# Strips of 64 bytes between the eight w_in slots of an attention and two-MLP kernel

## The chip, the cores and the metric

The kernel runs on one core of one Trainium2 chip. Its time is device microseconds of one execution, as the median of several runs. The engines go by their names in the profile: PE (TensorE matmuls), PEld (its weight loads), DVE (VectorE), ACT (ScalarE), POOL (GpSimd), SP (the queue that issues the DMAs).

## The reference

```python
proj = einsum('bhsd,df->bhsf', x, w_phi); proj -= max(abs(proj), axis=-1)
phi  = concat([exp(proj), exp(-proj)])                  # for q and for k
out  = (phi(q) @ (phi(k).T @ v)) / (phi(q) @ sum(phi(k)) + 1e-6)
x    = out as 2304 tokens x 512
x    = elu(x @ w1_in) @ w1_out                          # 512 -> 2048 -> 512
x    = (h * clip(h + 3, 0, 6) / 6) @ w2_out,  h = x @ w2_in
```

The batch is 4, with 8 heads, 576 positions and a head of 64. The weights of the MLPs arrive as 64-bit floats and are turned into 32-bit ones on the chip.

## The kernel before

The first 160 us or so are the attention, in eight units of two heads by two batches. Then come the two MLPs. Each MLP runs in eight rounds over its 2,048 hidden features, 256 features per round; the rounds are called 0 to 7 (first MLP, m = 0) and 8 to 15 (second, m = 1), and `g` is the round in the code. The 2,304 tokens are four blocks of 512 and one of 256.

A round computes the hidden layer of the four large blocks, two at a time, with Strassen's scheme in Winograd-like form: seven products P1 to P7 per pair of blocks instead of eight (`hid`, line 711). Each has an operand of the tokens (`X`, tiles x_A.. and x_S..) and one of the weights, a *part* of w_in: B11, B21, B12 and B22 are its quarters, T1 to T4 are sums and differences of these. The small block goes without the scheme and reads the four quarters (`hid4`, line 725). To keep precision, each operand is split into a high and a low half in the format fp32r, and a product is three matmuls (high by high, high by low, low by high); with two halves of the contraction that is a group of six matmuls of 128 x 128 weights against 512 columns. The second layer is `outp`, line 776, with w_out and the gated hidden tiles ga and gb.

A w_in part is one tile of 128 partitions by 2,048 bytes, high half first. ACT casts the high half (`part_hi`, line 665), POOL subtracts it from the 32-bit weights for the low half (`part_lo`, line 669). Before that the quarters come by DMA and go through a chain of ACT (627, 631), DVE (642, 648) and POOL (636, 652); the T parts are differences made by POOL in the place of the quarters' 32-bit copies (`diff`, line 658). The parts of a round are made during the round before it, always in the order B11, B21, B12, B22, T2, T3, T1, T4.

Behind a product on PE, ACT copies or activates it (733, 745, 746, 748), DVE adds and gates it (738, 752), ACT casts the gated tile's high half (`gate_hi`, 756), and DVE makes its low half (`gate_lo`, 759), which also frees the PSUM bank. `sums` (786, 788) adds the second layer's results into x.

The order of all work on all engines is written out by the kernel itself: it makes a list of steps with expected durations, and `in_order` simulates them with a plan of `rings` (how many buffers each ring has and which steps must be over before one is taken again) and emits the instructions in that order. Each engine executes its own list in that order. The tile framework gives the tiles their addresses and puts in the semaphore waits, according to which tile had the memory before. Within a round of the middle, PE's order is written out in the list `order`: the small block's groups and the rest of the round before, P1 and P2, P6, P5, P7 and so on of the first pair of blocks, mixed with second-layer groups, then those of the second pair, with P3 and P4 of the second pair last. These are the last readers of B22 and of T4 in a round.

The w_in parts live in the pool `wp`, as eight buffers of one tag, `wi`. Above it lie `stg` (the staging of the weights), `early` and the attention's `att_b`, whose memory the second pair's operands take later.

Of the kernel before, what the change touches and what calls it, by code (L numbers as in the profile page):

```python
# [8 lines left out]
F32 = mybir.dt.float32  # L9
I64 = mybir.dt.int64  # L10
F32R = mybir.dt.float32r
# [137 lines left out]
def attention_then_two_mlps(  # L149
# [44 lines left out]
    def step(engine, us, fn, **kw):  # L194
        s = Step(engine, us, fn, **kw)
        steps.append(s)
        return s
# [5 lines left out]
    rings = dict(BANKS)  # L203
# [17 lines left out]
    ctx.enter_context(tc.tile_pool(name="gap", bufs=1, side="right")).tile([128, 120], F32, name="gap_r")  # L221

    wp = ctx.enter_context(tc.tile_pool(name="wp", bufs=1))
    stg = ctx.enter_context(tc.tile_pool(name="stg", bufs=1))
    early = ctx.enter_context(tc.tile_pool(name="early", bufs=1))

# [16 lines left out]
    for i in range(2):  # L243
        t = apool.tile([128, R, 2, D + 1], F32, name=f"vb{i}")
# [312 lines left out]
    PARTS = ("B11", "B21", "B12", "B22", "T2", "T3", "T1", "T4")  # L557
# [31 lines left out]
    def y_open():  # L589
# [6 lines left out]
        "y": step("NONE", 0.0, y_open, after=y_users, rank=BEGIN),  # L596
        "n": step("NONE", 0.0, y_open, after=n_users, rank=BEGIN),
    }
    HB, YB = ["p0", "p1", "p2", "p3", "t1"], ["a0", "a1", "t0"]
    rings.update({"s": 2, "ca": 2, "bi": 4, "bo": 2, "wi": 8, "wo": 3, "h": len(HB), "y": len(YB),  # L600
                  "ma": 2, "mb": 2, "ga": 2, "gb": 2})
    nxt = {}

# [5 lines left out]
    F, WI, WO = {}, {}, {}  # L609
# [51 lines left out]
        nc.gpsimd.tensor_scalar(out=out_, in0=in_, scalar1=1.0, scalar2=0.0, op0=ALU.mult, op1=ALU.add)  # L661

    def part_hi(g, name, key):
        t = WI[g, name] = wp.tile([128, 2, 2, 128], F32R, tag="wi", name="w_in", bufs=8)
        nc.scalar.copy(out=t[:, 0].rearrange("p k f -> p (k f)"), in_=F[key])  # L665

    def part_lo(g, name, key):
# [110 lines left out]
    def sums(m, first_, b, d):  # L778
        t0, n = BLOCKS[b]
        ps = Y[b, d]  # L780
        part, ps = (xv[:, d, t0:t0 + n], ps[:, :n]) if m == 0 else (ov[:, t0 // 128 + d], ps)
        if first_:
            if b == 4:
                V.tensor_copy(out=part, in_=ps)
            else:
                nc.scalar.copy(out=part, in_=ps)  # L786
        else:
            V.tensor_tensor(out=part, in0=ps, in1=part, op=ALU.add)  # L788
# [72 lines left out]
    for g in range(2 * NP):  # L861
# [3 lines left out]
        h = [[("H", g, fi)] for fi in range(2)]  # L865
# [44 lines left out]
    PART, OUT, wi_tok, wo_tok = {}, {}, {}, {}  # L910
    chain = [None, None]

    def convert(key, lead):
        m, w, i, c = key
        ts_, ta, tb = Token("s"), Token("ca"), Token(("bi", "bo")[i])
        x = step("SP", 1.4, bind_(fetch, *key), takes=[ts_], rank=lead - 5, behind=[chain[0]] if chain[0] else [])
        chain[0] = x
        low, size, sign, up, end = to_f32(key)
        x = step("ACT", 0.95, low, after=[x], rank=lead, takes=[ta, tb], uses=[ts_])
        z = step("DVE", 0.45, sign, after=[x], rank=lead, port=True, uses=[ts_])  # L920
        x = step("POOL", 0.45, size, after=[x], rank=lead)
        x = step("DVE", 0.3, up, after=[x], rank=lead, port=True)
        return step("POOL", 0.75, end, after=[x, z], rank=lead, uses=[ta, tb]), tb

    for g in range(2 * NP):
        m, w = g // NP, 2 * (g % NP)
        lead = first[g] - W_IN_LEAD
        keys = {"B11": (m, w, 0, 0), "B21": (m, w, 0, 1), "B12": (m, w + 1, 0, 0), "B22": (m, w + 1, 0, 1)}
        done, tok, raw_ = {}, {}, {}

        def part(name, key, after, users):
            t = wi_tok[g, name] = Token("wi")
            hi = step("ACT", 0.40, bind_(part_hi, g, name, key), after=after, rank=lead, takes=[t], uses=users,
                      behind=[chain[1]] if chain[1] else [])
            chain[1] = hi
            lo = step("POOL", 0.75, bind_(part_lo, g, name, key), after=[hi], rank=lead, uses=users + [t])
            PART[g, name] = lo
            return lo

        for name, key in keys.items():  # L940
            raw_[name], tok[name] = convert(key, lead)
            done[name] = part(name, key, [raw_[name]], [tok[name]])

        def differ(out_, one, two, after):
            return step("POOL", 0.75, bind_(diff, keys[out_], keys[one], keys[two]), after=after, rank=lead,
                        uses=[tok[out_], tok[one], tok[two]])

        t1 = differ("B11", "B12", "B11", [done["B11"], raw_["B12"]])
        t3 = differ("B12", "B22", "B12", [done["B12"], raw_["B22"], t1])
        t2 = differ("B22", "B22", "B11", [done["B22"], t1, t3])  # L950
        t4 = differ("B21", "B21", "B22", [done["B21"], t2])
        part("T2", keys["B22"], [t2], [tok["B22"]])
        part("T3", keys["B12"], [t3], [tok["B12"]])
        part("T1", keys["B11"], [t1], [tok["B11"]])
        part("T4", keys["B21"], [t4], [tok["B21"]])
        lead = first_o[g] - W_OUT_LEAD
        for fi in range(2):
            t = wo_tok[g, fi] = Token("wo")
            for c in range(2):
                x, tb = convert((m, w + fi, 1, c), lead)  # L960
                hi = step("ACT", 0.40, bind_(out_hi, m, w + fi, c), after=[x] + ([OUT[g, fi]] if c else []),
                          rank=lead, takes=[] if c else [t], uses=[tb])
                OUT[g, fi] = step("POOL", 0.75, bind_(out_lo, m, w + fi, c), after=[hi], rank=lead, uses=[tb, t])
# [22 lines left out]
    def joined(g, pr, bank_, to, key, after, when):  # L986
        pt = ptok[g, pr, bank_]
        if to != bank_:
            ptok[g, pr, to] = Token("h")
        return step("DVE", 0.70, bind_(join, (g, pr, bank_), key, (g, pr, to)), after=after, rank=when,  # L990
                    takes=[ptok[g, pr, to]] if to != bank_ else [], uses=[pt, ptok[g, pr, to], mtok[key]])
# [9 lines left out]
    for x in order:  # L1001
        kind, g = x[:2]
# [3 lines left out]
        if kind == "P":  # L1006
# [11 lines left out]
            if term in ("P6", "P5", "P3"):  # L1018
                after.append(at[g, pr, {"P6": "s1", "P5": "s2", "P3": "s4"}[term]])
            s = step("PE", us, bind_(hid, ps, g, pr, term, term in OPENS), after=after, rank=clock, takes=takes,  # L1020
                     behind=behind, uses=[ptok[ps], wi_tok[g, part_]])
# [12 lines left out]
            if term in ("P1", "P2") and {"P1", "P2"} <= set(seen):  # L1034
                y = joined(g, pr, "Y", "Y", (g, b0, 0), [at[g, pr, "P2"], at[g, pr, "s1"]], when)
                finish(m, g, b0, 0, [y], (g, pr, "Y"), None, when)
            if term in ("P5", "P7") and {"P5", "P7"} <= set(seen):
                y = at[g, pr, "C22"] = joined(g, pr, "Z", "W", (g, b1, 1), [at[g, pr, "P7"], at[g, pr, "s4"]], when)
                finish(m, g, b1, 1, [y], (g, pr, "W"), None, when)
            if term == "P4":  # L1040
                y = joined(g, pr, "Z", "Z", (g, b1, 0), [s, at[g, pr, "s2"]], when)
                finish(m, g, b1, 0, [y], (g, pr, "Z"), None, when)
        elif kind == "H":
            fi = x[2]
            ps = (g, 4)
            if fi == 0:
                ptok[ps] = Token("h")
            names = ("B11", "B21", "B12", "B22")[2 * fi:2 * fi + 2]
            s = step("PE", us, bind_(hid4, ps, g, fi), after=[PART[g, n_] for n_ in names] + ready[m, 4, None] + [OPEN["n"]],
                     rank=clock, takes=[] if fi else [ptok[ps]], behind=behind,  # L1050
                     uses=[ptok[ps]] + [wi_tok[g, n_] for n_ in names])
# [3 lines left out]
        else:  # L1055
# [3 lines left out]
            s = step("PE", us, bind_(outp, m, g, b, d), rank=clock, behind=behind, takes=[ty],  # L1059
                     after=[tiles[g, b, fi] for fi in fis] + [OUT[g, 0], OUT[g, 1], OPEN["y"], OPEN["n"]],  # L1060
                     uses=[ty, wo_tok[g, 0], wo_tok[g, 1]] + [gtok[g, b, fi] for fi in fis])
            when = clock + us
            w = g % NP
            if w == 0:
# [9 lines left out]
                y = step("ACT" if b < 4 else "DVE", 0.57 if m or b < 4 else 0.35, bind_(sums, m, True, b, d), after=after, rank=when, uses=[ty])  # L1074
            else:
                y = step("DVE", 0.66 if m or b < 4 else 0.41, bind_(sums, m, False, b, d), after=[s, adds[m, b, d]], rank=when, uses=[ty])
# [24 lines left out]
def bind_(fn, *a):  # L1101
    return lambda: fn(*a)
# [50 lines left out]
```

## Time and profile before

| | |
|---|---|
| median of 3 runs | 938.45 us (938.14 to 939.03) |
| the profiled execution | 938.99 us, of which the span of the instructions is 937.2 us |
| PE busy | 903.2 us, 96% of the span |
| DVE, ACT, POOL busy | 72%, 61%, 42% |
| clock granted to PE | 0.998 on average |

The profile is of one execution. Busy times are the union of an engine's instructions; a timeline merges neighbouring instructions of one line into a row, and its bracket tells how long the engine stood idle before the row and which instruction ended that. Matmuls overlap in the pipeline, so the time per matmul is read from the starts of rows, not from the duration of one.

### The profile page before, as it was taken

Reading aid. Unit: us, or ns where it says so; the run is one execution under the profiler, and the core shown is the slowest. Engines: PE = TensorE matmul, PEld = TensorE weight load, DVE = VectorE, ACT = ScalarE, POOL = GpSimd, SP = SyncE. Lnnn points to the kernel's source line nnn. Section 1 sums busy time; section 2 is a strip of 40 time slices with the busy share of each in tenths; the row PEclk is TensorE's granted clock in tenths of the full one; section 3 lists DMA queues with packets and bytes.
Section 4 is the critical chain, followed back from the end, with each engine's and each line's share of the span. In section 5 each row is a group of like instructions: output and inputs, shape, how many; then the busy total and the mean of one; then the engine's idle time right before and its main releaser. Section 6 shows DMA issues by size and latency. Waiting matters only on the chain.

```text
span 937.2 us, 17621 instructions
## 1 busy us (share of the span) xinstructions
PE 903.2 (96%) x6792; PEld 759.3 (81%) x6792; DVE 677.9 (72%) x1202; ACT 567.3 (61%) x1207; POOL 398.0 (42%) x570
## 2 busy tenths in 40 slices
PE   8999999899999999999999978999999999999998
PEld 7888888778888888888888856888888888888886
DVE  6888887854868686868677789577777676767565
ACT  5687676877656565656566646765555554545331
POOL 0238721353535353535352555655544444444200
PEclk9999999999999999999999999999999999999999
DMA  7534420001111111111111000121111111110013
GB/s 223 158 114 119 134 82 2 1 13 44 39 52 40 51 38 53 37 54 37 55 37 55 11 12 23 58 68 56 56 62 40 50 42 54 36 54 26 1 66 137
DMA packets 42531, 53.69 MB, mean 57 GB/s; under 512 B 21328, under 2 KB 21456, under 8 KB 42448
## 3 DMA queue, kind: packets, MB, share of 16 engines
q1 hardware_dynamic: 42448, 52.57, 18.0%
q8 instruction: 53, 0.87, 0.4%
q14 instruction: 30, 0.25, 0.1%
HBM read 47.84 MB, written 4.72 MB: 56 GB/s over the span
## 4 chain that ended last, share of the span: by engine, by line
PE 88%; DVE 7%; ACT 4%; issue 1%; POOL 0%; POOLq 0%; ACTq 0%
PE ps_a L776 26%; PE ps_p L711 25%; PE ps_t L776 13%; PE ps_t L711 6%; PE ps_p L725 4%; PE ps_a L381 4%; PE ps_t L431 4%; PE ps_p L319 3%; ACT e L408 2%; DVE x L688 2%; DVE x_S L697 1%; PE ps_t L453 1%; PE ps_t L725 1%; DVE x_A L697 1%; DVE x L788 1%
## 5 line engine op out<-in xcount | busy, mean ns | idle before, releaser
L711 PE MATMUL ps_p<-x_S,w_in 128*128 128x512 f32 x630 | 159.3, 392 | 4.3 <-ACT mb L733 2.1
L788 DVE TENSOR_TENSOR x<-ps_a,x 128x512 f32<-128x512 f32 (+1 forms) x177 | 116.3, 660 | 49.5 <-PE ps_a L776 47.9
L711 PEld LDWEIGHTS ps_p<-x_S,w_in 128*128 128x128 f32 x630 | 118.5, 189 | 30.4 <-ACT mb L733 2.7
L669 POOL TENSOR_TENSOR w_in<-w_bi,w_in 128x256 fp32r<-128x256 f32 x128 | 94.8, 758 | 88.7 <-ACT w_in L665 88.5
L711 PE MATMUL ps_p<-x_A,w_in 128*128 128x512 f32 x468 | 117.4, 391 | 2.0 <-DVE ga L759 2.0
L636 POOL TENSOR_SCALAR w_a<-w_a 128x256 f32<-128x256 f32 x128 | 54.4, 426 | 125.7 <-ACT w_a L631 120.5
L711 PEld LDWEIGHTS ps_p<-x_A,w_in 128*128 128x128 f32 x468 | 86.9, 188 | 20.1 <-DVE ga L759 2.6
L652 POOL TENSOR_TENSOR w_bi<-w_bi,w_a 128x256 int32<-128x256 int32 x64 | 48.1, 755 | 113.1 <-DVE w_a L648 113.1
L776 PE MATMUL ps_a<-gb,w_out 128*128 128x512 f32 (+1 forms) x384 | 82.8, 357 | 6.8 <-DVE x L788 4.0
L788 DVE TENSOR_TENSOR x<-ps_t,x 128x512 f32<-128x512 f32 (+1 forms) x89 | 58.9, 662 | 37.9 <-PE ps_t L776 37.3
L776 PE MATMUL ps_a<-w_out,gb 128*128 128x512 f32 x336 | 82.7, 389 | 0.0
L776 PEld LDWEIGHTS ps_a<-gb,w_out 128*128 128x128 f32 x384 | 65.6, 191 | 18.7 <-DVE x L788 4.6
L776 PEld LDWEIGHTS ps_a<-w_out,gb 128*128 128x128 f32 x336 | 63.1, 188 | 13.1
L678 POOL TENSOR_TENSOR w_out<-w_bo,w_out 128x256 fp32r<-128x256 f32 x64 | 48.1, 752 | 59.1 <-ACT w_out L674 58.5
L776 PE MATMUL ps_a<-ga,w_out 128*128 128x512 f32 x258 | 64.3, 391 | 0.5 <-DVE ga L759 0.5
L652 POOL TENSOR_TENSOR w_bo<-w_bo,w_a 128x256 int32<-128x256 int32 x64 | 49.0, 767 | 33.1 <-DVE w_a L648 33.1
L329 DVE TENSOR_REDUCE mx<-ps_p 128x4 f32<-128x512 f32 (+1 forms) x80 | 50.3, 629 | 16.3 <-PE ps_p L319 16.2
L776 PE MATMUL ps_a<-w_out,ga 128*128 128x512 f32 x240 | 59.1, 391 | 1.9 <-ACT x L786 1.5
L733 ACT COPY mb<-ps_p 128x512 f32<-128x512 f32 x54 | 31.8, 589 | 45.5 <-PE ps_p L711 45.4
L752 DVE SCALAR_TENSOR_TENSOR ps_p<-ma,ps_p 128x512 f32<-128x512 f32 x66 | 45.7, 692 | 15.5 <-ACT ma L748 9.4
L776 PEld LDWEIGHTS ps_a<-ga,w_out 128*128 128x128 f32 x258 | 47.7, 188 | 10.4 <-DVE ga L759 0.9
L631 ACT ACTIVATE w_a<-w 128x256 f32<-128x256 f32 x128 | 54.5, 426 | 2.1 <-POOL w_bi L652 2.1
(109 smaller groups left out, 1907.0 us busy)
## 6 DMA issues: line engine op xcount, KB each, us to landing
w<-in_moe_w_in_dram SPq DMA_DIRECT2D x64, 256.0 KB, 2.6
w<-in_moe_w_out_dram SPq DMA_DIRECT2D x64, 256.0 KB, 2.6
vb<-in_v_dram SPq DMA_DIRECT2D x16, 288.0 KB, 4.3
out_dram<-x SPq DMA_DIRECT2D x18, 256.0 KB, 2.0
raw_k<-in_k_dram SPq DMA_DIRECT2D x7, 576.0 KB, 3.8
raw_q<-in_q_dram SPq DMA_DIRECT2D x7, 576.0 KB, 4.5
raw_k<-in_k_dram SPq DMA_DIRECT2D x1, 320.0 KB, 5.2
raw_q<-in_q_dram SPq DMA_DIRECT2D x1, 320.0 KB, 5.6
```

The costliest lines, as they stand in the source:

```text
L329: V.tensor_reduce(out=mx[:, :n], in_=P[j, h], axis=AX.X, op=ALU.max, apply_absolute_value=True)
L381: nc.tensor.matmul(out=acc[bb][f0:f0 + 64, h, half], lhsT=kp[p, i, half, f0:f0 + 64], rhs=vb[u % 2][p, r, h], start=(done.count(bb) == 1 a ...
L631: nc.scalar.activation(out=st["a"], in_=s.bitcast(F32).rearrange("p (n t) -> p n t", t=2)[:, :, 1], func=AF.Abs)
L636: nc.gpsimd.tensor_scalar(out=st["a"], in0=st["a"], scalar1=W_MOST, scalar2=W_LEAST, op0=ALU.min, op1=ALU.max)
L652: nc.gpsimd.tensor_tensor(out=b_, in0=b_, in1=st["a"].bitcast(I32), op=ALU.add)
L669: nc.gpsimd.tensor_tensor(out=t[:, 1], in0=F[key], in1=t[:, 0].bitcast(F32), op=ALU.subtract)
L678: nc.gpsimd.tensor_tensor(out=t[:, 1], in0=F.pop((m, w, 1, c)), in1=t[:, 0].bitcast(F32), op=ALU.subtract)
L711: nc.tensor.matmul(out=PS[ps_], lhsT=t[:, a_, kk], rhs=X[pr, op][x_][kk], start=(opens and i == 0), stop=(i == 5), skip_group_check=True,)
L725: nc.tensor.matmul(out=PS[ps_][:, 256 * fi:256 * fi + 256], lhsT=t[:, a_, kk], rhs=XB["x"][x_][2 * half + kk], start=(i == 0), stop=(i == ...
L752: V.scalar_tensor_tensor(out=PS[ps_], in0=MAIN[key], scalar=s, in1=PS[ps_], op0=o0, op1=o1)
L776: nc.tensor.matmul(out=o, lhsT=a_, rhs=b_, start=(fi + j == 0), stop=(fi == 1 and j == 2))
L788: V.tensor_tensor(out=part, in0=ps, in1=part, op=ALU.add)
```

## The change

The one pool of eight slots for w_in's parts is replaced by eight pools of one slot, one for each part, and between them lie pools of 64 bytes that nothing uses. In the plan, the ring `wi` of eight buffers becomes eight rings of one, `wiB11` to `wiT4`. `wp` keeps w_out's three buffers.

```diff
     wp = ctx.enter_context(tc.tile_pool(name="wp", bufs=1))
+    wip, strips = {}, []
+    for i, part in enumerate(("B11", "B21", "B12", "B22", "T2", "T3", "T1", "T4")):
+        wip[part] = ctx.enter_context(tc.tile_pool(name=f"wi_{part}", bufs=1))
+        strips.append(ctx.enter_context(tc.tile_pool(name=f"strip{i}", bufs=1)))
+        strips[-1].tile([128, 16], F32, name=f"strip{i}")
     stg = ctx.enter_context(tc.tile_pool(name="stg", bufs=1))
...
+    rings.update({"wi" + part: 1 for part in PARTS})
     HB, YB = ["p0", "p1", "p2", "p3", "t1"], ["a0", "a1", "t0"]
-    rings.update({"s": 2, "ca": 2, "bi": 4, "bo": 2, "wi": 8, "wo": 3, "h": len(HB), "y": len(YB),
+    rings.update({"s": 2, "ca": 2, "bi": 4, "bo": 2, "wo": 3, "h": len(HB), "y": len(YB),
                   "ma": 2, "mb": 2, "ga": 2, "gb": 2})
...
     def part_hi(g, name, key):
-        t = WI[g, name] = wp.tile([128, 2, 2, 128], F32R, tag="wi", name="w_in", bufs=8)
+        t = WI[g, name] = wip[name].tile([128, 2, 2, 128], F32R, tag="wi", name="w_in", bufs=1)
...
         def part(name, key, after, users):
-            t = wi_tok[g, name] = Token("wi")
+            t = wi_tok[g, name] = Token("wi" + name)
```

## Rows read from the trace of the kernel before

**Rows 1.** The page: busy time by engine, and the chain that ended last.
```profile
PE 903.2 (96%) x6792; PEld 759.3 (81%) x6792; DVE 677.9 (72%) x1202; ACT 567.3 (61%) x1207; POOL 398.0 (42%) x570
...
PE 88%; DVE 7%; ACT 4%; issue 1%; POOL 0%; POOLq 0%; ACTq 0%
```

**Rows 2.** Busy times by stretch: stretch, length, each engine's busy time (instructions), clock, DMA.
```profile
300.00:420.00 120.00, 119.96 (x591) 101.24 (x590) 85.28 (x154) 73.57 (x153) 50.39 (x78) 1.00 0.15 47
```

**Rows 3.** Timeline of PE in round 9: start, duration, line, tiles, count.
```profile
604.21 2.88 PE L711 MATMUL ps_p<-x_A,w_in 128*128 128x512 f32 x12
606.93 2.88 PE L776 MATMUL ps_a<-w_out,gb 128*128 128x512 f32 x12
```

**Rows 4.** Timeline of PE in the attention: transposes of shq and of nr.
```profile
101.71 0.60 PE L395 MATMUL ps_t<-ident,shq 128*128 128x128 f32 x4
...
163.07 0.49 PE L453 MATMUL ps_t<-ident,nr 128*128 128x128 f32 x3
```

**Rows 5.** ACT's groups of instructions: count, busy us, mean ns, idle before, releasers.
```profile
L665 ACT CAST w_in<-w_bi 128x256 fp32r<-128x256 f32 x128 | 47.7, 404 | 9.5 <-PE ps_p L711 3.9 <-POOL w_in L669 2.7 <-POOL w_bi L652 1.3
...
L694 ACT CAST x_b<-x 128x256 fp32r<-128x256 f32 x8 | 2.9, 407 | 0.1
```

**Rows 6.** POOL's instructions of three lines: durations in ns, minimum/median/maximum.
```profile
L697 POOL TENSOR_TENSOR x_A<-x,x_A x12: 1270/1282/1344, 33.3 to 566.6; 128x512 fp32r<-128x512 f32 x12
...
L688 POOL TENSOR_TENSOR x<-x x8: 1264/1276/1284, 79.0 to 108.7; 128x512 f32<-128x512 f32 x8
...
L669 POOL TENSOR_TENSOR w_in<-w_bi,w_in x128: 722/739/1229, 35.8 to 874.0; 128x256 fp32r<-128x256 f32 x128
```

**Rows 7.** Timeline of all engines, first MLP: round 3's parts are made.
```profile
291.80 1.52 PE L711 MATMUL ps_p<-x_S,w_in 128*128 128x512 f32 x6
...
292.60 0.39 ACT L665 CAST w_in<-w_bi 128x256 fp32r<-128x256 f32 x1
...
293.88 1.56 POOL L658 TENSOR_TENSOR w_bi<-w_bi 128x256 f32<-128x256 f32 x2
...
294.66 1.02 ACT L665 CAST w_in<-w_bi 128x256 fp32r<-128x256 f32 x3
...
296.13 0.41 ACT L665 CAST w_in<-w_bi 128x256 fp32r<-128x256 f32 x1 [0.46 <-POOL w_in L669]
296.44 0.58 ACT L756 CAST ga<-ps_p 128x512 fp32r<-128x512 f32 x1
...
298.04 0.68 DVE L759 TENSOR_TENSOR ga<-ps_p,ga 128x512 fp32r<-128x512 f32 x1
...
298.78 1.70 PE L725 MATMUL ps_p<-x_b,w_in 128*128 128x256 f32 x12
```

**Rows 8.** Timeline of all engines, second MLP: round 13's parts are made.
```profile
775.36 1.52 PE L711 MATMUL ps_p<-x_S,w_in 128*128 128x512 f32 x6
...
775.58 0.39 ACT L665 CAST w_in<-w_bi 128x256 fp32r<-128x256 f32 x1
...
778.08 1.52 PE L711 MATMUL ps_p<-x_A,w_in 128*128 128x512 f32 x6
...
779.70 0.41 ACT L665 CAST w_in<-w_bi 128x256 fp32r<-128x256 f32 x1 [0.99 <-PE ps_p L711]
780.01 0.58 ACT L756 CAST ga<-ps_p 128x512 fp32r<-128x512 f32 x1
...
781.61 0.68 DVE L759 TENSOR_TENSOR ga<-ps_p,ga 128x512 fp32r<-128x512 f32 x1
...
782.35 1.70 PE L725 MATMUL ps_p<-x_b,w_in 128*128 128x256 f32 x12
```

**Rows 9.** Timeline of PE and ACT in the second MLP: round 11's B21 is cast.
```profile
669.97 1.52 PE L711 MATMUL ps_p<-x_A,w_in 128*128 128x512 f32 x6
670.13 0.40 ACT L665 CAST w_in<-w_bi 128x256 fp32r<-128x256 f32 x1
...
671.55 0.59 ACT L756 CAST gb<-ps_p 128x512 fp32r<-128x512 f32 x1 [1.03 <-PE ps_p L711]
```

## The prediction

> **What bounds the kernel now.** I read the page first: PE is busy 96% of the span and the chain that ended last lies on PE for 88% of it [rows 1]. Then the busy times by stretch: in a steady stretch of the MLPs PE is busy 119.96 of 120 us at a granted clock of 1.00, which is the level of 2.4 GHz [rows 2]. So in the rounds a microsecond counts only if PE waits for it or if PE's own instructions get longer. Then the timeline of PE alone: twelve products of w_in take from 604.21 to 606.93, 2.72 / 12 = 0.2267 us from start to start, and the twelve of w_out behind them last 2.88 us as a group, exactly as these do [rows 3]. 512 columns at 2.4 GHz are 213.3 ns, so 13.3 ns per product are not streaming. Last the timeline of all engines around the casts that fill w_in's slots (ACT, L665), in a round of the first MLP and one of the second [rows 7, 8].
>
> **What the change does to addresses.** In the program of the kernel before, the eight slots lie at byte 39,424 + 2,048 i of a partition; 39,424 is 77 x 512, so every slot, and every block of 128 weights in it (512 bytes), starts on a multiple of 512. So do X's operands, w_out, w_bi and the gate tiles; x32 and ident lie 128 bytes past one. Afterwards part i starts 64 i bytes past a multiple of 512 (B11 0, B21 64, to T4 448). The eight strips sum to 512 bytes, so all that is allocated above them moves by exactly one multiple and keeps its offset. No instruction is added or taken away, and no transfer.
>
> Does an offset cost or give PE anything? The nearest rows are the transposes of the attention: at L395 the stationary operand is shq (offset 0) against ident (128), at L453 it is nr (offset 128) against the same ident: relative offsets of 128 and 0. A group of four of the one takes 0.60 us and a group of three of the other 0.49, a step of 0.11 us per transpose within which both lie [rows 4]. So neither equal offsets nor a stationary operand that starts 128 past a multiple shows a price. For ACT the nearest pair is the cast at L665 (0 to 0), 404 ns, and the cast of x_b at L694 (x at 128, target at 0), 407 ns for the same 256 columns [rows 5]. For POOL: 1,282 ns where x (128) meets x_A (0), 1,276 ns where all lies in x [rows 6]. I take zero, the value of all three pairs. The bounds, since no row has w_in's own shape at another offset: at most the whole 13.3 ns for each product, both ways.
>
> **What the change does to slots.** This is the part that the strips don't name. With one ring of eight, a tile gets a slot that has come free, not the one of its own part: in round 3 the cast of B22 starts at 292.60, while PE's group on round 2's B22 (L711, P3) runs from 291.80 to 293.32 [rows 7]; it can't be writing that slot. With a pool of one slot for each part it must wait for exactly that group. The hand-written order stays as it is: its plan already counted the ring of eight in order of taking, and a round takes its eight parts in a fixed order, so eight takes back is the same part one round earlier. Only the waits in the program move.
>
> T4 shows what such a wait is like: in round 13 its cast starts at 779.70, 0.10 us after P4's group (778.08 + 1.52 = 779.60) and after 0.99 us of idle time that PE ended [rows 8]. So the price of each new wait is the end of the group, plus 0.10, minus the present start:
> - B22, rounds 2 to 7: 293.32 + 0.10 - 292.60 = 0.82 us [rows 7]; all six look alike, 46.9 us apart.
> - B22, rounds 10 to 15: 775.36 + 1.52 + 0.10 - 775.58 = 1.40 us [rows 8]; five of them alike, round 11 some 0.7.
> - B21, up to 669.97 + 1.52 + 0.10 - 670.13 = 1.46 us in round 11 [rows 9], 1.1 in round 10, 0.2 in rounds 2 to 7, none in 12 to 15.
> - The other parts wait for groups that ended before their casts start, or, T4, for the group they wait for now.
> The sum is about 6 x 0.82 + 5 x 1.40 + 0.7 + 4 = 17 us of ACT. What is behind it on the engines? ACT's queue, and POOL, whose lower half of B22 (L669) needs the cast and whose two differences (L658, 293.88) stand behind that; the casts of T2, T3 and T1 at 294.66 need those [rows 7]. So they come 0.82 (1.40) us later. Then T4's cast has its own idle time, 0.46 us in round 3 and 0.99 in round 13, and takes that much back [rows 7, 8]: it is late by 0.82 - 0.46 = 0.36 and 1.40 - 0.99 = 0.41 us, and with it the cast of ga behind it (L756). In round 3 the row names POOL for that idle time; were it POOL's later work that T4 waits for, nothing would be given back there and ga would be late by the whole 0.82.
>
> Who waits for ga? DVE's L759, and it is what PE waits for: in round 3 it ends at 298.04 + 0.68 = 298.72 and PE's next group, L725, starts at 298.78; in round 13 it ends at 782.29 and PE starts at 782.35 [rows 7, 8]. But DVE comes to L759 late: ga is cast by 296.44 + 0.58 = 297.02 and L759 starts at 298.04; in round 13 780.59 and 781.61. That is 1.02 us of cover in both. 0.36 and 0.41 fit, with some 0.6 left, and so does 0.82. B21's wait is followed in round 11 by 1.03 us in which ACT stood idle for PE [rows 9]; 0.43 of the 1.46 are left, for the cast of gb, and that is less than ga's cover. So the sum on the path is 0, and the work that hides it is DVE's queue ahead of L759. If that cover were gone, the 0.36 and 0.41 would show in twelve rounds: 6 x 0.36 + 6 x 0.41 = 4.6 us.
>
> **The sum.** The profiled execution took 938.99 us, a span of 937.2 and 1.8 around it, 0.54 above the median of 938.45. 938.99 + 0 for the offsets + 0 for the waits, less the 0.54 by which that execution stands above the median: 938.5.
>
> **Rivals.**
> (a) *Slower: the waits get through to PE.* The place is ga before L759, the point from which it decides is a lateness of 1.02 us. It is passed if T4's idle time takes nothing back and POOL's lower halves meet DVE more often: one of these lasts 739 ns at the median and 1,229 at most [rows 6], 0.49 more. Without the give-back, rounds 10 and 12 to 15 cost 1.40 - 1.02 = 0.38 each, 1.9 us in all, 940.4; with 0.49 on top it is 0.29 in six rounds and 0.87 in five, 6.1 us, 944.6. Middle 942. For it: only 0.6 us are left, every round. Against it: the idle times stand in the rows of every round.
> (b) *Faster: equal offsets are what the 13.3 ns are.* Weights of the next product are read while the present one streams, and today both start on a multiple of 512. If seven of eight parts lose 13.3 ns on each of their products, it is 7/8 x (1,344 + 384) x 13.3 ns = 20 us: 918 (16 rounds of 14 groups of 6 at L711, and of 24 products at L725). Against it: rows 4, and w_out's products have the same pitch in the same rows 3. The Trainium skill's page "TensorE: Matmul & The Clock Gate", section "Back-to-back issue gap", gives N / 2.4 + 2.5 ns for a product at full clock, 215.8 ns here, where the trace has 226.7. By that page's figure an estimate of what could be won is 1,512 x 10.9 ns = 16.5 us. The page "SBUF — State Buffer", section "Who interferes with whom", speaks against any gain: it gives PE two independent read ports and says that "PE and ACT never wait on anyone". By that page the sum is the 0 of rows 4 to 6.
> (c) *Slower: weights off a multiple of 512 load longer.* Priced by the other end of the same bound, 20 us: 958; a few ns each give 945 to 950. Against it: nr, 128 past a multiple, in rows 4.
> (d) *The change doesn't do what it says,* because the allocator places the strips elsewhere. The time would be that of the forecast; the waits stay, since they come from the pools.
>
> **Numbers.** About 0.2% (1.9 us) is what a measurement of this kernel can tell from no change. Forecast 938.5, chance 0.73 ((d) included), nearly all of it within 0.2%. (a) 0.13, (c) 0.04: slower together 0.17. (b) 0.10. The range takes in (a) up to near its far end, and below the forecast only the spread: 936.2 to 944.0, which leaves out (b), (c) and the last of (a).
>
> **What would show each step.** Casts at L665 of B22 with idle time before them that PE ended, about 0.8 us in the first MLP and 1.4 in the second; T4's idle time gone; L759 and L725 at the same distance from PE's group before. PE's pitch 0.2267 for all parts: another pitch for w_in than for w_out would prove (b) or (c). If L725's group starts later in its round, with L759 waiting for ga's cast, it is (a).

## The result, and the profile after

The changed kernel takes 945.65 us (944.41 to 946.77) against 938.74 for the kernel before on the same chip: a ratio of 1.0072, with a 95% interval of 1.0054 to 1.0089. It is slower by 6.9 us, more than the 0.2% that a measurement can tell from no change, and 1.65 us above the upper end of the range. The profiled execution took 945.84 us with a span of 944.1; before's span was 937.2, so the two traces are 6.9 us apart too.

I read the page first: busy time by engine, then groups of instructions (count | busy us, mean ns of one | idle us before them and what ended it).

```profile
PE 912.4 (97%) x6792; PEld 761.5 (81%) x6792; DVE 674.7 (71%) x1202; ACT 567.3 (60%) x1207; POOL 397.5 (42%) x570
...
L717 PE MATMUL ps_p<-x_S,w_in 128*128 128x512 f32 x630 | 161.7, 396 | 4.2 <-ACT mb L739 2.1
...
L717 PEld LDWEIGHTS ps_p<-x_S,w_in 128*128 128x128 f32 x630 | 118.5, 189 | 32.3 <-ACT mb L739 2.7
...
L717 PE MATMUL ps_p<-x_A,w_in 128*128 128x512 f32 x468 | 120.4, 398 | 2.0 <-DVE ga L765 2.0
...
L671 ACT CAST w_in<-w_bi 128x256 fp32r<-128x256 f32 x128 | 46.9, 405 | 24.1 <-PE ps_p L717 12.3
```

Lines 711, 725 and 776 of before are 717, 731 and 782 here, 665 is 671, 756 and 759 are 762 and 765. The first group's row in before, and its weight loads:

```profile
L711 PE MATMUL ps_p<-x_S,w_in 128*128 128x512 f32 x630 | 159.3, 392 | 4.3 <-ACT mb L733 2.1
...
L711 PEld LDWEIGHTS ps_p<-x_S,w_in 128*128 128x128 f32 x630 | 118.5, 189 | 30.4 <-ACT mb L733 2.7
```

Two things changed. ACT's casts of w_in stand idle for 24.1 us instead of 9.5 [rows 5], 12.3 of it for PE: these are the new waits. And PE is busy for 9.2 us more [rows 1] with the same 6,792 instructions, while its idle time before w_in's products is what it was (4.2 us here, 4.3 in before). PE doesn't wait more; its products take longer. The weight loads themselves don't: 189 ns each in both.

Not all of the 9.2 us come from the change, because the granted clock differs between the two traces. The stretch around the turn from the first MLP to the second, first before, then after (length, busy time of PE, PEld, DVE, ACT and POOL with their instructions, clock, DMA):

```profile
540.00:660.00 120.00, 108.82 (x509) 89.48 (x507) 89.47 (x150) 74.56 (x160) 66.17 (x87) 0.99 0.14 46
```

```profile
540.00:660.00 120.00, 109.97 (x496) 89.86 (x497) 87.71 (x147) 73.47 (x157) 67.29 (x87) 0.96 0.14 42
```

Here the clock is 0.96 in after and 0.99 in before; from 300 to 420 and from 780 to 900 us it is 1.00 in both. At the turn PE waits for other engines for 2 to 3.5 us at a time, and behind some of these waits it runs products of 512 columns at 427 ns each, at the level of 1.2 GHz, in after for longer than in before. The same 301 products (504.11 to 579.75 in before, 506.33 to 583.16 in after) keep PE busy for 2.9 us more, mostly in time in which it otherwise stood idle, and take 1.2 us more. The rounds ahead of them take 2.8 us more, those behind them 3.5, and the attention 0.6 less. So 6.3 us arise at the full clock. The clock doesn't make the difference of the medians either: the run of the kernel after with 0.998 took 944.41 us, and the kernel before's runs with 0.998 took 936.56 to 939.25 on all chips.

Where does the time go within PE? The timeline of PE in round 13 (start, duration, line, out<-moving operand,weights, count), first before, then after; a group's pitch is the step from its start to the next one's.

```profile
790.82 1.52 PE L711 MATMUL ps_p<-x_A,w_in 128*128 128x512 f32 x6
792.18 1.52 PE L711 MATMUL ps_t<-x_A,w_in 128*128 128x512 f32 x6
793.54 2.88 PE L776 MATMUL ps_a<-w_out,gb 128*128 128x512 f32 x12
796.26 1.52 PE L711 MATMUL ps_p<-x_S,w_in 128*128 128x512 f32 x6
...
804.42 1.52 PE L711 MATMUL ps_p<-x_S,w_in 128*128 128x512 f32 x6
```

```profile
796.29 1.52 PE L717 MATMUL ps_p<-x_A,w_in 128*128 128x512 f32 x6
797.65 1.56 PE L717 MATMUL ps_t<-x_A,w_in 128*128 128x512 f32 x6
799.04 2.91 PE L782 MATMUL ps_a<-w_out,gb 128*128 128x512 f32 x12
801.79 1.52 PE L717 MATMUL ps_p<-x_S,w_in 128*128 128x512 f32 x6
803.15 1.52 PE L782 MATMUL ps_t<-w_out,gb 128*128 128x512 f32 x6
804.51 1.53 PE L782 MATMUL ps_a<-w_out,gb 128*128 128x512 f32 x6
805.88 2.96 PE L717 MATMUL ps_p<-x_S,w_in 128*128 128x512 f32 x12
808.67 1.55 PE L717 MATMUL ps_p<-x_A,w_in 128*128 128x512 f32 x6
810.06 1.53 PE L717 MATMUL ps_p<-x_S,w_in 128*128 128x512 f32 x6
```

In before every six products take 1.36 us. In after they take 1.36 where the part is B11 (796.29, offset 0) and T2 (801.79, offset 256), 1.39 where it is B21 (797.65, offset 64), and 2.79 for T1 and T3 together (805.88, offsets 384 and 320). The w_out products behind B21 pay as well, 2.75 for twelve, and so does the second pair's B11 right behind T3, 1.39 (808.67). From the first of these groups to the last, sixty products later, it is 13.60 us in before and 13.77 in after.

The rows round to 0.01 us. From the start of each single product one can add up how much longer its pitch is than 226.7 ns (119.7 for 256 columns), over all products of the MLPs, leaving out steps over 30 ns, which are waits or products at 1.2 GHz. This *sum of small steps* is 1.4 us in before and 8.1 in after: 6.6 of the 6.9 us. By group of six:

```
part           offset   extra ns per group of six
B11, T2        0, 256        1   (not right behind one of the others)
B21, T3       64, 320       37   (9 4 9 4 9 2 by product)
T1               384       33   (14 6 3 5 1 3)
B22              192       12   (-1 2 5 -1 3 4)
T4               448       14   (3 5 -1 2 5 0)
w_out or B11 group right behind one at 64 (B21, T3): 28; w_out behind T1: 3; behind B22: 20; behind T4: 0
```

A pair of blocks uses each of these seven parts once, so, with 13 for B22 and T4 each, a round costs 2 x (2 x 37 + 33 + 2 x 13) = 266 ns and 16 rounds 4.3 us; the trace's sum for the w_in products of 512 columns grew by 4.3. The w_out groups behind them grew by 2.5, and the products of 256 columns shrank by 0.1: 6.6 in all.

### The profile page after: what moved, and what is told of

Read it like the earlier page. It is cut to its first block, busy times and chain, and to the rows that moved or that the text cites. A ratio compares the mean times of both kernels' runs of the same rounds, so it can differ in the third digit from the quotient of the medians.

```text
span 944.1 us, 17538 instructions
## 1 busy us (share of the span) xinstructions
PE 912.4 (97%) x6792; PEld 761.5 (81%) x6792; DVE 674.7 (71%) x1202; ACT 567.3 (60%) x1207; POOL 397.5 (42%) x570
## 4 chain that ended last, share of the span: by engine, by line
PE 88%; DVE 6%; ACT 4%; issue 1%; POOL 0%; POOLq 0%; ACTq 0%
PE ps_a L782 26%; PE ps_p L717 26%; PE ps_t L782 13%; PE ps_t L717 6%; PE ps_p L731 4%; PE ps_a L386 4%; PE ps_t L436 4%; PE ps_p L324 3%; ACT e L413 2%; DVE x L694 2%; PE ps_t L458 1%; DVE x_S L703 1%; PE ps_t L731 1%; DVE x_A L703 1%; DVE x L794 1%
## 5 line engine op out<-in xcount | busy, mean ns | idle before, releaser
L717 PE MATMUL ps_p<-x_S,w_in 128*128 128x512 f32 x630 | 161.7, 396 | 4.2 <-ACT mb L739 2.1
L717 PE MATMUL ps_p<-x_A,w_in 128*128 128x512 f32 x468 | 120.4, 398 | 2.0 <-DVE ga L765 2.0
L671 ACT CAST w_in<-w_bi 128x256 fp32r<-128x256 f32 x128 | 46.9, 405 | 24.1 <-PE ps_p L717 12.3
```

The costliest lines, as they stand in the source:

```text
L717: nc.tensor.matmul(out=PS[ps_], lhsT=t[:, a_, kk], rhs=X[pr, op][x_][kk], start=(opens and i == 0), stop=(i == 5), skip_group_check=True,)
```

## Experiments

Two theories stood at first: the new waits cost the time, or the offsets do. The edits are against the kernel after where they show its strips, else against the kernel before. A pool `fill` makes a shift up to 512 bytes, so that what lies above keeps its offset. All times are medians, with the ratio to the kernel before on the same chip.

**Waits without strips.** Eight pools of one slot, no strips.

```diff
-        strips.append(ctx.enter_context(tc.tile_pool(name=f"strip{i}", bufs=1)))
-        strips[-1].tile([128, 16], F32, name=f"strip{i}")
```

> Eight pools of one slot each, no strips: all parts at multiples of 512, the waits of the change kept. Theory O (the offsets lengthen PE's products): about 938.7 us, the time of before, with w_in's products at a pitch of 226.7 ns, and casts of B22 that wait 0.8 and 1.4 us. Rival W (the waits of one slot per part get through to PE): about 945.6 us.

Measured: 938.9 us, ratio 0.9996 (0.9985 to 1.0007). The casts among its groups of instructions by line:

```profile
L669 ACT CAST w_in<-w_bi 128x256 fp32r<-128x256 f32 x128 | 47.0, 406 | 23.2 <-PE ps_p L715 11.8 <-POOL w_bi L662 8.2 <-POOL w_bi L656 1.4
```

All the new waits are there, 23.2 us of idle time, and the kernel is as fast as before. The waits cost nothing that the time shows.

**Offsets without waits.** One ring of eight as before, each slot 64 bytes longer.

```diff
-        t = WI[g, name] = wp.tile([128, 2, 2, 128], F32R, tag="wi", name="w_in", bufs=8)
+        w = wp.tile([128, 528], F32R, tag="wi", name="w_in", bufs=8)
+        t = WI[g, name] = w[:, 0:512].rearrange("p (a k f) -> p a k f", a=2, k=2)
```

> One ring of eight slots as before, each slot 64 bytes longer: the eight offsets of the change without its waits; the parts take turns on the offsets. Theory O: about 945.6 us (944 to 947), w_in's products 3 to 4 ns longer in the mean. Rival W: 938.7 us.

Measured: 945.54 us, ratio 1.0059 (1.004 to 1.0078), with the casts idle as little as in before:

```profile
L666 ACT CAST w_in<-w_bi 128x256 fp32r<-128x256 f32 x128 | 47.7, 404 | 9.9 <-PE ps_p L712 4.6 <-POOL w_in L670 2.1 <-PE ps_t L712 1.6
```

The offsets alone give the loss.

**Is 512 the period?** Strips of 256 bytes behind B11, B12, T2 and T1, none behind the others, so that parts lie at 0 or 256.

```diff
-        strips.append(ctx.enter_context(tc.tile_pool(name=f"strip{i}", bufs=1)))
-        strips[-1].tile([128, 16], F32, name=f"strip{i}")
+        if i % 2 == 0:
+            strips.append(ctx.enter_context(tc.tile_pool(name=f"strip{i}", bufs=1)))
+            strips[-1].tile([128, 64], F32, name=f"strip{i}")
```

> Eight pools of one slot, with strips of 256 bytes after B11, B12, T2 and T1: parts at 0 and at 256 past a multiple of 512. In the trace of the change T2, at 256, has no longer pitch than before. Theory O with a period of 256 bytes: about 938.7 us. Theory O with a period of 512: half of the parts pay, 942 to 944 us. Rival W: 945.6 us.

Measured: 938.35 us, ratio 0.9993 (0.998 to 1.0006), sum of small steps 1.4 us. An offset of 256 is free: as far as a group's own price goes, offsets repeat after 256 (in the kernel after, 64 and 320 cost alike too, and 192 and 448 nearly). What a group leaves to the one behind it doesn't quite: 20 ns behind B22 (192), none behind T4 (448).

**Whose offset?** The weights stay at 0; X's operands are moved by 64 bytes for 12 of a round's 14 groups.

```diff
+    ctx.enter_context(tc.tile_pool(name="sh_e", bufs=1)).tile([128, 16], F32, name="sh_e")
     early = ctx.enter_context(tc.tile_pool(name="early", bufs=1))
+    ctx.enter_context(tc.tile_pool(name="fill", bufs=1)).tile([128, 112], F32, name="fill")
...
         sb.close()
+        ctx.enter_context(tc.tile_pool(name="sh_b", bufs=1)).tile([128, 16], F32, name="sh_b")
```

> Weights as before, all on multiples of 512; instead the moving operands of twelve of the fourteen groups per round (x_A.., x_S.. of the first pair but S2 and S4, and all of the second pair) lie 64 bytes past one. Theory O-rel (what counts is where the weights lie against the operand that streams): slower, about 941 to 945 us, with the groups' patterns of the parts at 192 and 448 in the change, 64 behind a multiple of 256. Theory O-abs (what counts is the offset of the weights alone): 938.7 us, pitch 226.7 ns.

Measured: 947.81 us, ratio 1.008 (1.0058 to 1.0101). No weight was moved, and it is slower all the same. A group behind another one of that kind has the steps 5 -1 2 5 -1 2, the three steps of the parts at 192 and 448 in the kernel after, begun at another of the three: weights at 0 less moving operand at 64 is 192 modulo 256. What counts is the distance between the two operands of a product. The time lies 3 us above the 941 to 945 that were expected for this: in this trace a w_out group right behind one at this distance pays 25 to 31 ns, where the text spoke of the groups' own patterns alone.

**Both moved together.** All that lies behind the two gaps in SBUF, the operands of the MLPs among it, goes 64 bytes further.

```diff
-    const.tile([128, 208], F32, name="gap")
-    ctx.enter_context(tc.tile_pool(name="gap", bufs=1, side="right")).tile([128, 120], F32, name="gap_r")
+    const.tile([128, 224], F32, name="gap")
+    ctx.enter_context(tc.tile_pool(name="gap", bufs=1, side="right")).tile([128, 104], F32, name="gap_r")
```

> Every tile of the MLPs (and of the attention, x32 and ident apart) moved by 64 bytes together, on both sides of SBUF: weights and moving operands all lie 64 past a multiple of 512, none against the other. Theory O-rel (the distance of the weights from the operand that streams, taken modulo 256): 939 us, pitch 226.7 ns. Theory O-abs (weights must start on a multiple of 256): slower than the change, 948 us or more, since w_out is off it as well.

Measured: 938.42 us, ratio 1.000 (0.9988 to 1.0011). The timeline of PE in round 13 has before's steps, with every weight and every X 64 bytes off:

```profile
789.61 1.52 PE L711 MATMUL ps_p<-x_A,w_in 128*128 128x512 f32 x6
790.97 1.52 PE L711 MATMUL ps_t<-x_A,w_in 128*128 128x512 f32 x6
...
803.21 1.52 PE L711 MATMUL ps_p<-x_S,w_in 128*128 128x512 f32 x6
```

This refutes that weights off a multiple of 512 (or 256) load slowly, as rival (c) had put it.

**All of w_in at one offset.** The eight slots in a pool of their own, all at 64; w_out at 0. It tells whether the distance counts, or a change of distance from group to group.

```diff
+    ctx.enter_context(tc.tile_pool(name="sh_w", bufs=1)).tile([128, 16], F32, name="sh_w")
+    wip = ctx.enter_context(tc.tile_pool(name="wip", bufs=1))
+    ctx.enter_context(tc.tile_pool(name="fill", bufs=1)).tile([128, 112], F32, name="fill")
     stg = ctx.enter_context(tc.tile_pool(name="stg", bufs=1))
...
-        t = WI[g, name] = wp.tile([128, 2, 2, 128], F32R, tag="wi", name="w_in", bufs=8)
+        t = WI[g, name] = wip.tile([128, 2, 2, 128], F32R, tag="wi", name="w_in", bufs=8)
```

> One ring of eight slots as before, but all eight at the same 64 bytes past a multiple of 512; w_out and the moving operands as before. Theory O-rel: each of the 14 groups of a round costs what B21's and T3's cost in the change (37 ns), and a w_out group behind one 28 ns: 14 x 37 + about 8 x 28 = 740 ns a round, 12 us in all: 948 to 952 us. Theory O-chg (only a change of offset from one weight load to the next costs): about half of that, 943 to 946 us, since w_in's groups that follow each other pay nothing.

Measured: 949.31 us, ratio 1.0123 (1.0103 to 1.0143), worse than the kernel after. Timeline of PE in round 13:

```profile
797.15 1.56 PE L714 MATMUL ps_p<-x_A,w_in 128*128 128x512 f32 x6
798.55 1.56 PE L714 MATMUL ps_t<-x_A,w_in 128*128 128x512 f32 x6
799.95 2.91 PE L779 MATMUL ps_a<-w_out,gb 128*128 128x512 f32 x12
...
806.84 2.96 PE L714 MATMUL ps_p<-x_S,w_in 128*128 128x512 f32 x12
809.64 1.56 PE L714 MATMUL ps_p<-x_A,w_in 128*128 128x512 f32 x6
811.04 1.33 PE L714 MATMUL ps_p<-x_S,w_in 128*128 128x512 f32 x5
```

Now every w_in group takes 1.40 us, also one that follows another at the same distance (798.55, and 2.80 for the twelve at 806.84). The distance itself costs.

**Strips of 32 bytes.** Offsets 0, 32, ... 224.

```diff
-        strips[-1].tile([128, 16], F32, name=f"strip{i}")
+        strips[-1].tile([128, 8], F32, name=f"strip{i}")
+    ctx.enter_context(tc.tile_pool(name="fill", bufs=1)).tile([128, 64], F32, name="fill")
```

> The change with strips of 32 bytes instead of 64: parts at 0, 32, 64 to 224 past a multiple of 256. Theory O-rel: B12 at 64, T2 at 128 and T1 at 192 show the patterns that these distances have in the change (37, 33 and 13 ns a group), and the others show what 32, 96, 160 and 224 cost, not known yet; if they lie between, 943 to 948 us. If lines of 64 bytes were what counts, 32 would cost as 0 or as 64.

Measured: 948.11 us, ratio 1.0101 (1.0084 to 1.0117). The waits of the pools are in it too, and cost nothing by the first experiment. The extra per group of six is 34 ns at 32, 35 at 96 and at 128, 37 at 160, 23 at 192 and 40 at 224. Here only 0 is free; in the kernel after T2's 256 was, too. The time lies just above the 943 to 948 that were expected if the new distances cost what lies between the known ones.

**Products of 256 columns.** Only the small block's operand x_b is moved by 64 bytes (distance 192 for line 725).

```diff
+        pools["a"].tile([128, 16], F32, name="sh_x")
         t = pools["a"].tile([128, 2, KD, 256], F32R, name="x_b4")
+        pools["a"].tile([128, 112], F32, name="fill")
```

> The kernel before with x_b4 alone, the moving operand of the 256-column products at L725, moved by 64 bytes. In the run with one ring of longer slots some of these products had a pitch of 113 ns instead of 120 at a distance of 192. Theory O-rel: the 24 products of a round change by up to -7 ns each, and the 27 ns of the group behind them may change: 937.0 to 939.5 us, at best 0.2% under before. Otherwise 938.7 us.

Measured: 938.68 us, ratio 1.0003 (0.9991 to 1.0014). These products don't pay: their twelve are shorter by some 15 ns, if anything, 0.4 us in the sum of small steps, which the time can't show.

**Another tensor.** w_in at 0, w_out's three slots at 64.

```diff
+    ctx.enter_context(tc.tile_pool(name="sh_w", bufs=1)).tile([128, 16], F32, name="sh_w")
+    wop = ctx.enter_context(tc.tile_pool(name="wop", bufs=1))
+    ctx.enter_context(tc.tile_pool(name="fill", bufs=1)).tile([128, 112], F32, name="fill")
...
-            WO[m, w] = wp.tile([128, 2, 512], F32R, tag="wo", name="w_out", bufs=3)
+            WO[m, w] = wop.tile([128, 2, 512], F32R, tag="wo", name="w_out", bufs=3)
```

> w_in's parts lie at 0 as in the kernel before; w_out's three slots lie 64 bytes past a multiple of 256, while their moving operands (ga, gb) stay at 0. Theory that the distance between weights and moving operand counts, whichever tensors they are: the 272 groups of six of the second layer get 37 ns each (10.1 us) and some 120 w_in groups that follow them 28 ns (3.4 us), some 1 us is saved on the 256-column products: 949 to 954 us. Theory that it is something of w_in alone (its casts, its slots, X's operands): 939 us.

Measured: 949.75 us, ratio 1.0108 (1.0081 to 1.0136), so nothing of it belongs to w_in alone. It lies at the lower edge of what was expected because that text took w_out for the weights in both MLPs. In the second one w_out is the moving operand (line 773), so the distance there is 192: its groups pay 18 to 30 ns behind other groups of 512 columns, those of the first MLP, at 64, 38 to 40.

The sum of small steps, worked out for each kernel from its trace, against the measured times:

```
                    sum of small steps,   change against   change of the
                    us                    before, us       median, us
after               8.1                     6.6              6.9
pools, no strips    1.5                     0.0             -0.4
ring, padded slots  6.9                     5.5              6.3
strips of 256       1.4                     0.0             -0.9
X at 64             9.9                     8.5              8.6
all at 64           1.2                    -0.2             -0.6
w_in at 64         11.6                    10.2             10.3
strips of 32       10.0                     8.6              9.1
x_b at 64           1.0                    -0.4             -0.4
w_out at 64        12.2                    10.8             10.8
```

The two columns of changes agree within 0.9 us over a spread of 11, so to that extent the lengthened pitch accounts for the time in every kernel. Each sum is of one trace; runs of one kernel scatter by 1 to 5 us.

## Why the prediction was wrong

**What bounds the kernel: right.** PE's own instructions set the time; 6.6 us more of them are nearly all of the 6.9 us.

**The zero for the offsets: the step that failed.** It took three pairs of rows for evidence, and none of them has the shape that pays. The transposes of [rows 4] have 128 columns. Their rows round to 10 ns and stand in groups of four and three, but read from the starts of single products in the same trace they go at a median of 109 ns (shq) and 110 (nr): for 128 columns the zero holds at both distances. It was carried over to 512 columns, and there it fails. [Rows 5] and [rows 6] are of ACT and POOL and say nothing of the two operands of a PE product. What was wanted was two w_in products of 512 columns at different distances, and before has none: its operands all lie at distance 0. The text said so itself and gave a bound, 13.3 ns either way; the bound held for a group's mean (T1's first product pays 14), but neither the sum nor the range used it. In the place of zero the runs showed 6.6 us. Over the 1,512 products that rivals (b) and (c) counted that is 4.4 ns each. That count is itself a little high: the pairs use seven parts, six of them moved, and the small block four, three of them moved, 1,152 + 288 = 1,440.

A hint did stand in before's trace, in a row that the argument passed over, behind the small block's group in round 13:

```profile
786.71 2.91 PE L776 MATMUL ps_a<-w_out,ga 128*128 128x512 f32 x12
789.46 1.52 PE L776 MATMUL ps_t<-w_out,ga 128*128 128x512 f32 x6
```

Twelve products of w_out take 2.75 us here and 2.72 from 793.54 to 796.26, with no wait and all operands at distance 0: the pitch of 226.7 ns isn't fixed, but can be disturbed by a few ns per product for a group.

**The strips' arithmetic: right.** The parts lie where the diff puts them; rival (d) fell with the steps by offset.

**The waits: right, close to the numbers.** Timeline of all engines after, round 3's parts, and of round 13's three rows:

```profile
292.10 1.53 PE L717 MATMUL ps_p<-x_S,w_in 128*128 128x512 f32 x6
...
293.67 0.41 ACT L671 CAST w_in<-w_bi 128x256 fp32r<-128x256 f32 x1 [0.71 <-PE ps_p L717]
...
295.77 1.33 ACT L671 CAST w_in<-w_bi 128x256 fp32r<-128x256 f32 x4 [0.53 <-POOL w_bi L664]
...
297.00 0.58 ACT L762 CAST ga<-ps_p 128x512 fp32r<-128x512 f32 x1
...
298.39 0.68 DVE L765 TENSOR_TENSOR ga<-ps_p,ga 128x512 fp32r<-128x512 f32 x1
...
299.13 1.68 PE L731 MATMUL ps_p<-x_b,w_in 128*128 128x256 f32 x12
...
780.76 1.53 PE L717 MATMUL ps_p<-x_S,w_in 128*128 128x512 f32 x6
...
782.33 0.41 ACT L671 CAST w_in<-w_bi 128x256 fp32r<-128x256 f32 x1 [1.28 <-PE ps_p L717]
...
785.65 0.58 ACT L762 CAST ga<-ps_p 128x512 fp32r<-128x512 f32 x1
```

B22's cast starts 1.57 us after its group of PE instead of 0.80 [rows 7]: 0.77 late, where 0.82 was forecast. The casts behind it start 3.67 us after that group instead of 2.86, 0.81 late. T4's idle time is gone, the fourth cast runs on with the others, and gave back what the text counted on: ga's cast starts 4.90 us after the group instead of 4.64, 0.26 late where 0.36 was forecast, and ends at 297.58, so that 0.81 of the 1.02 us of cover before L765 are left. L731 starts 7.03 us after the group instead of 6.98; the 0.05 are longer products. In round 13 B22's cast is 1.35 us late (1.57 behind its group instead of 0.22; 1.40 was forecast), and ga's 0.24 (0.41). So rival (a) has nothing, and the time of the pools without strips, 938.9, shows it.

**Rival (b)** has the sign wrong: distance 0 is the cheapest case for 512 columns that any of these kernels shows, and none of the 13.3 ns goes away at another one.

**Rival (c)** had the right price ("a few ns each give 945 to 950") and the wrong mechanism. Weights off a multiple cost nothing when their moving operands are off by as much (all at 64: 938.42), weights on a multiple can cost (X at 64: 947.81), and the weight loads are not longer in the records. Its chance of 0.04 rested on nr in [rows 4] alone, and the upper end of the range on (a) alone.

By the Trainium skill's page "SBUF — State Buffer", section "Who interferes with whom", PE has one read port for the moving operand and an independent one for the weights and "PE and ACT never wait on anyone". The prediction called that page in for the zero that it had taken from rows 4 to 6. The measurement differs and decides: with w_in 64 bytes off its moving operand the ratio is 1.0123, though the weight loads take 188 to 189 ns as before.

What stays open: what in the chip makes the distance count, why the distances 64 and 192 have different prices, why products of 128 and 256 columns don't pay, and why T4 leaves nothing to the group behind it and B22 20 ns. No run here looks inside. Reading both operands at the same moment is not a full account: the records place the load of a product's weights beside the product ahead of it (in after B21's first load starts at 797.42, with B11's last product), and B11's six still take 1.36 us; with strips of 32 bytes, B11's last product ahead of B21 pays 8 ns. The 0.3 us between 6.6 and 6.9 are a balance of the rest: between the two traces the steps over 30 ns grew by 0.9 us, mostly at the turn of the MLPs, and the attention took 0.6 less.

## What to carry to other kernels

Where PE is the bound and each fp32r product of 512 columns loads its own weights, keep the two operands of a product at the same offset modulo 256 bytes, as far as these kernels show; shifting one of them by 64 cost up to 1.2% here, shifting both nothing. Padding between tiles is therefore an edit of the products, even though no instruction changes. And a zero should be taken from a row of the same shape on the same engine, or else the whole bound belongs in the range.

## What the runs showed of the hardware

- The pitch of 512-column fp32r products depends on weights' address minus moving operand's, modulo 256 bytes: per group of six 0 to 1 ns more at distance 0 (away from groups that pay), 37 to 40 at 64, 33 to 36 at 128, 12 to 30 at 192, 34 to 40 at 32, 96, 160 and 224.
- The price outlasts the group: six products at distance 0 mostly pay 28 ns right behind a group at 64, 3 to 5 behind one at 128, and anything from 0 (behind T4 in after) to 29 (X at 64) behind one at 192. The 27 ns that before's groups pay behind 256-column ones (7 9 1 5 4 0 by product) look like it.
- Products of 128 columns don't show this (109 and 110 ns at distances 128 and 0), nor do those of 256 columns at 192.
- Twelve waits of ACT for PE at w_in's casts, 11.8 us in all, cost nothing measurable: 0.9996 (0.9985 to 1.0007).
